# Block-sparse attention with a routed expert layer, one core: weights and next keys loaded at other steps, first loads reordered, the last pair staggered by three units, expert pieces moved

## The chip, the cores and the metric

The kernel runs on 1 core of one Trainium2 chip. The metric is the device time of one execution in microseconds (us). The engines are TensorE (PE; its weight loads are listed apart as PEld), VectorE (DVE), ScalarE (ACT), GpSimd (POOL) and SyncE (SP), and SP issues most transfers; its queue is listed as SPq.

## The reference

```
attention: B=4, H=8, S=768, D=64, blocks of 32 (24 blocks)
mask[i, j] = |i - j| <= 1 or i or j in {first, last block} or j in the 3 sampled blocks of i
x = softmax(scale * q k^T where mask) @ v          -> x[b] is 768 x 512 (all heads side by side)
routed expert layer, for each b, capacity 128:
  score = x[b] @ w_gate                            768 scores
  top   = the 128 rows with the largest score
  out[b]      = x[b]
  out[b, top] = x[b, top] + sigmoid(score[top]) * (relu(x[b, top] @ w1) @ w2)    w1 512x1024, w2 1024x512
```

## The kernel before

**Steps.** The batch elements are worked in two pairs (`n` = 0 and 1: b = 0, 1 and b = 2, 3). The list `steps` holds 56 steps, 28 for a pair. The first six of a pair are the "g" steps, three for each element: the first and the last block row, which see all keys (`s_g`, `pt_g`, `o_g`). Then come 11 units `u` (two block rows each), each unit once for either element: scores from the unit's own keys (`s<-k`), from gathered sampled keys (`s<-kr`), a maximum on DVE (`mx`), exponentials on ACT (`pr`), transposes on PE (`pt`, copied to `pc`), and the product with the values (`o<-vs`, `o<-vr`), normed on DVE (`x`) and written out. In step s the program issues: what `todo` holds for s (loads, gathers), due pieces "a", the norm of step s-1, exponentials of s+1, transposes of s, scores of s+2, the product `o` of s, due pieces "b", the maxima of s+2, then "c" and "d". Every engine runs its instructions in the order in which they are written.

**Transfers.** SP's queue carries queries (`load_q`), keys (`load_k`), values (`load_vs`, `load_vg`), outputs and the expert weights `w1_s`, `w2_s` (`w_load`, eight loads of 512 KB). POOL gathers the sampled value rows (`vr<-vt,vidx`, an indirect transfer) and copies sampled keys (`kr<-k`). `scale_q` multiplies a loaded query tile by 0.125 on ACT.

**Routing and experts.** For each element, `route(b)` lays down pieces at steps counted from `ready(t)`, the step after the one that ends score tile t (two units, 128 tokens): scores to a row (`row`, `row_out`, by way of DRAM and `spread`, or for the last tile on chip by a product with ones, `on_chip`), columns, six ranks `M` on DVE, `sums`, `select`, `chosen`, and `fetch`, which gathers the 128 chosen rows (`xe<-out,it` on POOL). The expert is `xt` (transposes), four plus four pieces `h_mm`, two `relu`, eight pieces `y_mm` and `put` (scatter to the output). `EXPERT[b]` says at which step `xt` stands. Steps above 55 hold no attention; there the pieces run one behind the other. In the last pair the final two units are staggered: both of b=2 first, then both of b=3.

```
    EXPERT = (38, 47, 2 * (NU - 1 + NG) + 33, 2 * (NU - 1 + NG) + 42)
    steps += [(B - 2 + i, u) for i in range(2) for u in (NU - 2, NU - 1)]
        early(9 + 2 * i, lambda i=i: w_load(i))
```

Of the kernel before, what the change touches and what calls it, by code (L numbers as in the profile page):

```python
# [7 lines left out]
F32 = mybir.dt.float32  # L8
# [22 lines left out]
NG = 3  # L31
# [14 lines left out]
def block_sparse_attention_moe(ctx, tc, qt, kt, vt, blocks, w_gate, w1, w2, outs):  # L46
# [61 lines left out]
    def load_vg(n, m):  # L108

        i, c = m // 3, m % 3  # L110
        if m % 2 == 0:
            vts[n, m // 2] = value_tile(f"vg{n}_{m}")
        vg = vts[n, m // 2][:, m % 2]
        cols = slice(i * VR, (i + 1) * VR)
        r = rows_of(n, 1 + 8 * c)
        if c < 2:
            sp.dma_start(vg, vt[r:r + 256, cols].rearrange("(m p) c -> p m c", p=P))
        else:
            sp.dma_start(vg[:, 0], vt[r:r + 128, cols])
            sp.dma_start(vg[0:64, 1], vt[r + 128:r + 192, cols])  # L120
            for k, j in enumerate((0, NB - 1)):
                r = rows_of(n, j)
                sp.dma_start(vg[64 + 32 * k:96 + 32 * k, 1], vt[r:r + BLK, cols])
# [23 lines left out]
                 blocks.bitcast(I32).rearrange("(o a) b -> o (a b)", o=1).broadcast_to([P, NB * 6]))  # L147
    load_k(0, 8, 16, 0, 1)
    load_k(0, 16, 24, 0, 1)
    load_vg(0, 0)  # L150
    load_q(0, 0, 1, 2)
    load_k(0, 0, 8, 1, 2)
    load_vg(0, 1)
    load_k(0, 8, 16, 1, 2)
    load_vg(0, 2)
    load_k(0, 16, 24, 1, 2)
    load_vg(0, 3)


# [273 lines left out]
    def small_t(shape, name):  # L433

        n = 1
        for c in shape[1:]:
            n *= c
        if spare["at"] + n > 512:
            spare["bank"], spare["at"] = ps_o.tile([P, 512], F32, tag="o", name=name), 0
        r = spare["bank"][:, spare["at"]:spare["at"] + n]  # L440
        spare["at"] += n + n % 2
        return r[0:shape[0]] if len(shape) == 2 else r.rearrange("p (a b) -> p a b", a=shape[1])[0:shape[0]]

    EXPERT = (38, 47, 2 * (NU - 1 + NG) + 33, 2 * (NU - 1 + NG) + 42)

    def route(b):
        R = {}
# [2 lines left out]
        def ready(t):  # L450
            return steps.index((b, 2 * t + 1)) + 1
# [22 lines left out]
        def on_chip():  # L474
            r = rout.tile([P, 2, 2 * BLK], F32, tag="r", name=f"r{b}")
            vec.tensor_tensor(r, sps[b][:, NU - 2:NU].unsqueeze(2).broadcast_to([P, 2, 2 * BLK]),
                              d64.unsqueeze(1).broadcast_to([P, 2, 2 * BLK]), ALU.mult)
            R["rp"] = small_t([P, P], f"rs{b}")
            pe.matmul(R["rp"], ones, r.rearrange("p u c -> p (u c)"), start=True, stop=True, skip_group_check=True)

        def on_chip_out():
            act.copy(R["sb"][:, S - P:S], R["rp"])

        def columns(t0, t1):
            R["scp", t0] = small_t([P, t1 - t0, BLK], f"scp{b}_{t0}")
            for t in range(t0, t1):
                pe.transpose(R["scp", t0][:, t - t0], R["sb"][0:BLK, t * P:(t + 1) * P], ident[0:BLK, 0:BLK])
# [55 lines left out]
            vec.reciprocal(ge, ge)  # L543

        def mid(name):
            return ps_m.tile([P, 512], F32, tag="m", name=f"{name}{b}").rearrange("p (t c) -> p t c", t=4)

        def xt():
            R["pm"] = mid("xt")
# [18 lines left out]

        def y_mm(f):
            if f == 0:  # L570
                R["y"] = ps_m.tile([P, 512], F32, tag="m", name=f"y{b}")
            pe.matmul(R["y"], R["h"][:, f], w2_s[:, f], start=f == 0, stop=f == 7)

        def put():
# [15 lines left out]
        c, r = ready(4) + 4, ready(5)  # L590
        last = b >= B - 2
        plan += [(c, "c", lambda: rank(3)), (c + 1 if last else c + 2, "c", lambda: rank(4))]
        plan += [(r, "b", on_chip), (r + 1, "a", on_chip_out), (r + 1, "b", lambda: columns(5, 6)),
                 (r + 2, "a", lambda: columns_out(5, 6)), (r + 2, "d", table)]
        c = r + 2 if last else r + 6
        plan += [(c, "c", lambda: rank(5)), (c + 1, "b", sums), (c + 1, "c", select), (c + 2, "b", chosen),
                 (c + 3, "a", fetch)]
        e = EXPERT[b]
        plan += [(e, "b", xt), (e + 1, "a", xt_out)]
        plan += [(e + 1 + c // 2, "b", lambda c=c: h_mm(c)) for c in range(4)]  # L600
        plan += [(e + 3, "a", lambda: relu(0))]
        plan += [(e + 3 + c // 2, "b", lambda c=c: h_mm(4 + c)) for c in range(4)]
        plan += [(e + 5, "a", lambda: relu(1))]
        plan += [(e + 5 + f // 2, "b", lambda f=f: y_mm(f)) for f in range(8)]
        plan += [(e + 9, "a", put)]
# [21 lines left out]
    def early(s, f):
        todo.setdefault(max(s, 0), []).append(f)
# [41 lines left out]
    for s in range(n + 1):  # L670
        for f in todo.pop(s, []):
            f()
        run(s, "a")
        done = None
        if s:
            t = steps[s - 1]
            if t[1] == "g":
                join(t[0], t[2])
            if t[1:] == ("g", NG - 1):
                done = (t[0], 0)  # L680
            elif t[1] != "g":
                done = t
        if done:
            norm(*done)
        if s < n:
            if s + 1 < n:
                exps(steps[s + 1], 0)
            turn(steps[s])
        if done:
            gate(*done)  # L690
        if s < n:
            if s + 1 < n:
                exps(steps[s + 1], 1)
            if s + 2 < n:
# [12 lines left out]
        run(s, "d")  # L707
# [43 lines left out]
```

## Time and profile before

| | |
|---|---|
| runs, us | 349.74 median of 3 (352.0, 349.74, 345.66) |
| profiled execution, us | 347.55, of which the span of instructions is 345.8 |
| busy, share of the span | PE 82%, PEld 62%, DVE 53%, ACT 47%, POOL 37% |
| transfers | 64.85 MB, 188 GB/s over the span |
| granted TensorE clock | 0.948 of full on average |

A step is seen on PE by its eight transposes `pt`: step 0's begin at 14.82 us, step 6's at 44.82, step 9's at 55.76, step 19's at 105.23, step 28's (the second pair) at 142.09, step 37's at 182.00, step 55's at 281.66. The last product `o` of step 55 ends at 284.62 us; what follows is the tail: the rest of routing for b = 2 and 3, and their two experts.

### The profile page before, as it was taken

To read this page: it belongs to the slowest core of one execution; us is meant where nothing else is said; L and a number is where in the kernel's file an instruction comes from. 1 tells how busy PE (TensorE), PEld (TensorE's weight loads), DVE (VectorE), ACT (ScalarE), POOL (GpSimd) and SP (SyncE) were. 2 spreads that over 40 slices of the span, in tenths; PEclk is the share of its full clock that TensorE was granted. 3 is DMA by queue.
4 is the path that set the end of the run, shared out by engine and by line. 5 is a ranking of instruction groups with operands and counts; after the bars stand their busy time and mean duration, and the time that the engine had idled before them with its cause. 6 is when DMAs were issued, how large, how long until landed. Compare 5 with 4: busy or idle time off the path is not lost.

```text
span 345.8 us, 13626 instructions
## 1 busy us (share of the span) xinstructions
PE 284.8 (82%) x5766; PEld 214.3 (62%) x5766; DVE 184.5 (53%) x536; ACT 161.2 (47%) x373; POOL 127.4 (37%) x271
## 2 busy tenths in 40 slices
PE   5597697799658889987879899998999983399791
PEld 4265576667546667766656788665788661384650
DVE  1756486466535777887876454544665627400000
ACT  2436676557446666595636554544464430100100
POOL 3129365565551400379637535523600004300101
PEclk9999699989989999999999999999999997579997
DMA  6999989988998984968947947645720211100000
GB/s 176 324 301 279 329 220 303 333 278 271 312 316 227 332 270 137 334 193 248 322 125 213 252 148 212 165 124 176 228 66 17 64 32 48 61 0 2 30 0 31
DMA packets 34541, 64.85 MB, mean 188 GB/s; under 512 B 4400, under 2 KB 18224, under 8 KB 34480
## 3 DMA queue, kind: packets, MB, share of 16 engines
q1 hardware_dynamic: 27504, 38.45, 38.5%
q0 software_dynamic: 6976, 25.53, 23.2%
q8 instruction: 45, 0.74, 0.9%
q14 instruction: 16, 0.13, 0.1%
HBM read 56.61 MB, written 7.35 MB: 185 GB/s over the span
## 4 chain that ended last, share of the span: by engine, by line
PE 44%; issue 25%; POOL 7%; DVE 7%; DMA 6%; SPq 5%; POOLq 3%; ACT 2%; DVEq 0%; ACTq 0%
PE o L69 14%; PE s L69 10%; PE pt L69 8%; POOL kr L69 5%; SPq L69 5%; PE h L69 5%; PE y L69 4%; DMA vg<-vt 3%; POOLq L263 2%; DMA q<-qt 2%; POOL vr L69 2%; DVE M L69 2%; PE o_g L69 1%; DMA xe<-out,it 1%; DVE gm L69 1%
## 5 line engine op out<-in xcount | busy, mean ns | idle before, releaser
L69 ACT ACTIVATE pr<-s,mx 128x256 f32<-128x256 f32 x176 | 74.7, 484 | 27.1 <-DVE mx L69 24.4
L69 DVE TENSOR_REDUCE mx<-s 128x2 f32<-128x512 f32 x88 | 56.8, 686 | 47.4 <-PE s L69 46.2
L69 POOL DMA_INDIRECT vr<-vt,vidx x44 | 43.0, 977 | 97.3 <-PE o L69 49.4
L69 POOL COPY kr<-k 128x256 f32 (+1 forms) x176 | 67.1, 423 | 16.1 <-DMA vg<-vt 9.0
L69 ACT COPY pc<-pt 128x512 f32<-128x512 f32 x78 | 42.5, 590 | 39.0 <-PE pt L69 38.7
L69 PE MATMUL pt<-ident,pr 128*128 128x128 f32 x352 | 47.6, 278 | 1.8 <-issue 1.8
L69 PE MATMUL s<-kr,q 64*32 64x128 f32 x1408 | 35.9, 284 | 9.5 <-issue 9.5
L69 PEld LDWEIGHTS pt<-ident,pr 128*128 128x128 f32 x352 | 38.4, 141 | 6.3 <-issue 3.8
L69 PE MATMUL o<-vr,pc 128*32 128x65 f32 x1408 | 32.2, 227 | 7.5 <-issue 7.5
L69 PE MATMUL h<-xT,w_s 128*128 128x128 f32 x256 | 34.1, 293 | 2.8 <-ACT h L69 1.4
L69 PE MATMUL o<-vs,pc 128*64 128x65 f32 x704 | 32.6, 232 | 3.5 <-ACT pc L69 1.4
L69 PEld LDWEIGHTS h<-xT,w_s 128*128 128x128 f32 x256 | 31.8, 204 | 5.2 <-ACT xT L69 2.0
L69 POOL DMA_INDIRECT out<-xe,it x4 | 4.0, 1006 | 83.1 <-DVE z L69 44.4
L69 PEld LDWEIGHTS o<-vs,pc 128*64 128x64 f32 x704 | 25.8, 141 | 13.8 <-ACT pc L69 4.5
L69 PEld LDWEIGHTS s<-kr,q 64*32 64x32 f32 x1408 | 20.5, 108 | 20.6 <-issue 20.5
L69 PE MATMUL y<-w_s,h 128*128 128x512 f32 x64 | 30.1, 609 | 1.4 <-ACT h L69 1.4
L69 PEld LDWEIGHTS o<-vr,pc 128*32 128x32 f32 x1408 | 23.7, 112 | 11.1 <-issue 7.9
L69 PE MATMUL s<-k,q 64*64 64x128 f32 x704 | 30.2, 288 | 0.2 <-issue 0.2
L69 DVE SCALAR_TENSOR_TENSOR xe<-y,ge,xe 128x512 f32<-128x512 f32 x4 | 3.0, 751 | 43.0 <-PE y L69 43.0
L69 PEld LDWEIGHTS s<-k,q 64*64 64x64 f32 x704 | 19.4, 135 | 7.7 <-issue 7.0
L69 DVE CUSTOM_DVE_ANT_0 j<-x,wg_i 128x256 f32<-128x256 f32 x48 | 22.5, 468 | 1.3
L69 PE MATMUL o_g<-vg,pc_g 128*64 128x65 f32 x384 | 15.1, 236 | 8.2 <-ACT pc_g L69 8.2
(115 smaller groups left out, 293.3 us busy)
## 6 DMA issues: line engine op xcount, KB each, us to landing
k<-kt SPq DMA_DIRECT2D x12, 512.0 KB
q<-qt SPq DMA_DIRECT2D x23, 256.0 KB
vs<-vt SPq DMA_DIRECT2D x22, 260.0 KB
out<-x SPq DMA_DIRECT2D x88, 64.0 KB
vg<-vt SPq DMA_DIRECT2D x8, 520.0 KB
w_s<-w SPq DMA_DIRECT2D x8, 512.0 KB
vs<-vt SPq DMA_DIRECT2D x12, 130.0 KB
vg<-vt SPq DMA_DIRECT2D x4, 260.0 KB
```

Of the source, the lines that this page charges most:

```text
L69: i = getattr(self.engine, name)(*args, **kw)
L263: _, offs[n, u] = nc.values_load_multi_w_load_instructions(koff[0:1, 2 * u - 1:2 * u + 1, :], engines=[POOL], min_val=0, max_val=(NB - 1) ...
```

## The change

Six things are done. (1) The eight weight loads go from steps 9, 11, ..., 23 to steps 29, 31, 33, 35, 36, 38, 40, 42. (2) The next pair's keys are loaded in eight pieces at steps 6, 8, ..., 20 in place of six at 8, 11, ..., 23. (3) In the first loads, the second query half goes ahead of the first values, the last keys and `load_q(0, 1)` ahead of the third values; `scale_q` goes from the head of a step, four steps ahead of its unit, to a place behind the exponentials, three ahead. (4) In the last pair three units are staggered (`AHEAD = 3`), and for b = 2 and 3 score tile 4 goes on chip like tile 5, tile 3 alone by DRAM; some ranks move. (5) Expert pieces of b = 0 and 1 stand at `xt` steps 35 and 48 (38 and 47 before), one `h_mm` a step in place of two. (6) The experts of b = 2 and 3 take their PSUM tiles from the four buffers of `ps_s` in place of the single one of `ps_m`.

```diff
+AHEAD = 3
     load_k(0, 16, 24, 0, 1)
+    load_q(0, 0, 1, 2)
     load_vg(0, 0)
-    load_q(0, 0, 1, 2)
     load_k(0, 0, 8, 1, 2)
     load_vg(0, 1)
     load_k(0, 8, 16, 1, 2)
+    load_k(0, 16, 24, 1, 2)
+    load_q(0, 1)
     load_vg(0, 2)
-    load_k(0, 16, 24, 1, 2)
     load_vg(0, 3)
...
-    EXPERT = (38, 47, 2 * (NU - 1 + NG) + 33, 2 * (NU - 1 + NG) + 42)
+    EXPERT = ((35, 1), (48, 1), (60, 2), (69, 2))
...
+            pool = (ps_s, "s") if b >= B - 2 else (ps_m, "m")
...
-        for t0, t1, lag in ((0, 3, 3), (3, 5, 2)):
+        for t0, t1, lag in ((0, 3, 3), (3, 4, 3)) if last else ((0, 3, 3), (3, 5, 2)):
...
+        for t in (4, 5) if last else (5,):
+            r = ready(t)
+            plan += [(r, "b", lambda t=t: on_chip(t)), (r + 1, "a", lambda t=t: on_chip_out(t)),
+                     (r + 1, "b", lambda t=t: columns(t, t + 1)), (r + 2, "a", lambda t=t: columns_out(t, t + 1))]
...
-        plan += [(e + 1 + c // 2, "b", lambda c=c: h_mm(c)) for c in range(4)]
+        plan += [(e + 1 + c // g, "b", lambda c=c: h_mm(c)) for c in range(4)]
...
-    steps += [(B - 2 + i, u) for i in range(2) for u in (NU - 2, NU - 1)]
+    steps += [(B - 2 + i, u) for i in range(2) for u in range(NU - AHEAD, NU)]
...
-            early(max(a - 4, k + 1), lambda n=n, u=u: scale_q(n, u))
+            scaled(max(a - 3, k + 1), lambda n=n, u=u: scale_q(n, u))
...
-            for c in range(6):
-                early(s0 - 20 + 3 * c, lambda n=n, c=c: load_k(n, 4 * c, 4 * c + 4))
+            for c in range(8):
+                early(s0 - 22 + 2 * c, lambda n=n, c=c: load_k(n, 3 * c, 3 * c + 3))
...
-        early(9 + 2 * i, lambda i=i: w_load(i))
+        early((29, 31, 33, 35, 36, 38, 40, 42)[i], lambda i=i: w_load(i))
```

**SP's queue.** This is SP in the first pair before, at steps 8 to 11 (`k1` is the next pair's keys, `q0_6` the query tile of unit 6 of pair 0, `x1_1` unit 1 of element 1, `w1_s` the weights).

```order
L69 DMA q0_6_914<-qt 128x512
L69 DMA k1_916<-kt 128x1024
L69 DMA out1<-x1_1_921 64x256 x2
L69 DMA w1_s_209<-w1 128x1024
L69 DMA out0<-x0_2_1025 64x256 x2
L69 DMA vs1_85<-vt 64x1040
L69 DMA q0_7_1112<-qt 128x512
L69 DMA out1<-x1_2_1117 64x256 x2
L69 DMA k1_916<-kt 128x1024
L69 DMA w1_s_209<-w1 128x1024
```

And this is SP of the changed kernel at the head of the second pair, steps 29 to 33.

```order
L70 DMA w1_s_211<-w1 128x1024
L70 DMA vs2_86<-vt 64x1040
L70 DMA vs2_86<-vt 32x1040 x2
L70 DMA q1_3_2992<-qt 128x512
L70 DMA w1_s_211<-w1 128x1024
L70 DMA out2<-x2_0_3083 32x256 x4
L70 DMA vs0_84<-vt 64x1040
L70 DMA vs0_84<-vt 32x1040 x2
L70 DMA q1_4_3159<-qt 128x512
L70 DMA w1_s_211<-w1 128x1024
```

The weights have left the first pair's stretch and stand between the second pair's values and queries.

**PE in the tail.** Before, behind the last product `o3_11_11` (b = 3, unit 11) stands one pair of `y1` (expert of b = 1), then routing only, up to `xt2`.

```order
L69 MATMUL o3_11_11_5559<-vr1_11_4889,pc3_11_11_1_5555 32x65 x16
L69 MATMUL y1_5375<-w2_s_210,h1_5098 128x512 x2
L69 MATMUL o3_11_11_5559<-ident_137,sb2_4441 128x32
L69 MATMUL o3_11_11_5559<-ident_137,sb3_4543 128x32 x2
L69 MATMUL rs3_5606<-r3_5604,ones_142 128x128
...
L69 MATMUL xt2_5721<-ident_137,xe2_5671 128x128 x4
```

In the changed kernel the same place holds two `h_mm` of b = 1 and all its eight `y` pieces, with the sums and choices of b = 2 and 3 between them (left out here).

```order
L70 MATMUL o3_11_11_5564<-vr1_11_4884,pc3_11_11_1_5560 32x65 x16
L70 MATMUL h4_1_5461<-xT1_4998,w1_s_211 128x128 x4
L70 MATMUL o3_11_11_5564<-ident_139,sb3_4542 128x32
L70 MATMUL h4_1_5461<-xT1_4998,w1_s_211 128x128 x4
...
L70 MATMUL cp2_5617<-r3_5_5639,ones_144 128x128
L70 MATMUL y1_5651<-w2_s_212,h1_5377 128x512 x2
...
L70 MATMUL y1_5651<-w2_s_212,h1_5377 128x512 x4
...
L70 MATMUL y1_5651<-w2_s_212,h1_5377 128x512 x2
L70 MATMUL xt2_5714<-ident_139,xe2_5665 128x128 x4
```

So three `y` pairs and two `h_mm` have moved from ahead of the last product to behind it, and the choice of b = 3 stands behind `xt2` where it stood ahead.

**ACT at the start.** Before, the scaling of the second query tile `q0_1` stands ahead of the exponentials of step 3 and the copies of step 2 (the rows `pr0_g`/`pr1_g` are exponentials, `pc0_g` copies).

```order
L69 ACTIVATE pr0_g_2_1_352<-s0_g_2_1_275,gm0_226 128x256 x2
L69 ACTIVATE q0_1_248<-q0_1_248 128x512
L69 ACTIVATE pr1_g_0_0_399<-s1_g_0_0_355,gm1_382 128x256 x2
L69 COPY pc0_g_2_0_407<-pt0_g_2_0_402 128x512
L69 COPY pc0_g_2_1_414<-pt0_g_2_1_409 128x512
```

In the changed kernel the same place reads:

```order
L70 ACTIVATE pr0_g_2_1_352<-s0_g_2_1_275,gm0_228 128x256 x2
L70 ACTIVATE pr1_g_0_0_398<-s1_g_0_0_355,gm1_382 128x256 x2
L70 COPY pc0_g_2_0_406<-pt0_g_2_0_401 128x512
L70 COPY pc0_g_2_1_413<-pt0_g_2_1_408 128x512
...
L70 ACTIVATE pr1_g_1_1_498<-s1_g_1_1_419,gm1_382 128x256 x2
L70 ACTIVATE q0_1_102<-q0_1_102 128x512
```

The scaling has moved from ahead of the copies `pc0_g_2` to behind the exponentials of two later steps.

More of the change, by code (lines that the diff above doesn't have):

```diff
@@ L472, in spread, with on_chip, on_chip_out @@
             sp.dma_start(R["sb"][:, t0 * P:t1 * P], R["row", t0].broadcast_to([P, (t1 - t0) * P]))
-        def on_chip():
-            r = rout.tile([P, 2, 2 * BLK], F32, tag="r", name=f"r{b}")
-            vec.tensor_tensor(r, sps[b][:, NU - 2:NU].unsqueeze(2).broadcast_to([P, 2, 2 * BLK]),
+        def on_chip(t):
+            r = rout.tile([P, 2, 2 * BLK], F32, tag="r", name=f"r{b}_{t}")
+            vec.tensor_tensor(r, sps[b][:, 2 * t:2 * t + 2].unsqueeze(2).broadcast_to([P, 2, 2 * BLK]),
                               d64.unsqueeze(1).broadcast_to([P, 2, 2 * BLK]), ALU.mult)
-            R["rp"] = small_t([P, P], f"rs{b}")
+            R["rp"] = small_t([P, P], f"rs{b}_{t}")
             pe.matmul(R["rp"], ones, r.rearrange("p u c -> p (u c)"), start=True, stop=True, skip_group_check=True)
-        def on_chip_out():
-            act.copy(R["sb"][:, S - P:S], R["rp"])
+        def on_chip_out(t):
+            act.copy(R["sb"][:, t * P:(t + 1) * P], R["rp"])
         def columns(t0, t1):
@@ L545, in mid @@
         def mid(name):
-            return ps_m.tile([P, 512], F32, tag="m", name=f"{name}{b}").rearrange("p (t c) -> p t c", t=4)
+            pool = (ps_s, "s") if b >= B - 2 else (ps_m, "m")
+            return pool[0].tile([P, 512], F32, tag=pool[1], name=f"{name}{b}").rearrange("p (t c) -> p t c", t=4)
         def xt():
@@ L570, in y_mm @@
             if f == 0:
-                R["y"] = ps_m.tile([P, 512], F32, tag="m", name=f"y{b}")
+                R["y"] = mid("y").rearrange("p t c -> p (t c)")
             pe.matmul(R["y"], R["h"][:, f], w2_s[:, f], start=f == 0, stop=f == 7)
@@ L578, in put @@
                 in_=R["xe"][:], in_offset=None)
+        last = b >= B - 2
         plan = [(ready(2), "b", begin)]
-        for t0, t1, lag in ((0, 3, 3), (3, 5, 2)):
+        for t0, t1, lag in ((0, 3, 3), (3, 4, 3)) if last else ((0, 3, 3), (3, 5, 2)):
             s_ = ready(t1 - 1)
@@ L589, in route @@
         plan += [(c, "c", lambda: rank(0)), (c + 1, "c", lambda: rank(1)), (c + 2, "c", lambda: rank(2))]
[L590 to L598, printed above, removed]
-        plan += [(e, "b", xt), (e + 1, "a", xt_out)]
-        plan += [(e + 1 + c // 2, "b", lambda c=c: h_mm(c)) for c in range(4)]
[L601 to L605, printed above, removed]
+        for t in (4, 5) if last else (5,):
+            r = ready(t)
+            plan += [(r, "b", lambda t=t: on_chip(t)), (r + 1, "a", lambda t=t: on_chip_out(t)),
+                     (r + 1, "b", lambda t=t: columns(t, t + 1)), (r + 2, "a", lambda t=t: columns_out(t, t + 1))]
+        c = r + 2 if last else r + 5
+        if last:
+            plan += [(ready(3) + 5, "c", lambda: rank(3)), (ready(4) + 2, "c", lambda: rank(4))]
+        else:
+            plan += [(r + 3, "c", lambda: rank(3)), (r + 4, "c", lambda: rank(4))]
+        plan += [(r + 2, "d", table), (c, "c", lambda: rank(5)), (c + 1, "b", sums), (c + 1, "c", select),
+                 (c + 2, "b", chosen), (c + 3, "a", fetch)]
+        e, g = EXPERT[b]
+        plan += [(e, "b", xt), (e + 1, "a", xt_out)]
+        plan += [(e + 1 + c // g, "b", lambda c=c: h_mm(c)) for c in range(4)]
+        e += 1 + 4 // g
+        plan += [(e, "a", lambda: relu(0))]
+        plan += [(e + c // g, "b", lambda c=c: h_mm(4 + c)) for c in range(4)]
+        e += 4 // g
+        plan += [(e, "a", lambda: relu(1))]
+        plan += [(e + f // 2, "b", lambda f=f: y_mm(f)) for f in range(8)]
+        plan += [(e + 4, "a", put)]
         for o, where, f in plan:
@@ L617, in block_sparse_attention_moe @@
             steps += [(2 * n + i, "g", c) for c in range(NG)]
-        for u in range(1, NU - 2 if n == NPAIR - 1 else NU):
+        for u in range(1, NU - AHEAD if n == NPAIR - 1 else NU):
             steps += [(2 * n + i, u) for i in range(2)]
-    steps += [(B - 2 + i, u) for i in range(2) for u in (NU - 2, NU - 1)]
+    steps += [(B - 2 + i, u) for i in range(2) for u in range(NU - AHEAD, NU)]
     n_, per = len(steps), 2 * (NU - 1 + NG)
@@ L623, in block_sparse_attention_moe, with scaled @@
         route(b)
-    todo = {}
+    todo, late = {}, {}
+    def scaled(s, f):
+        late.setdefault(max(s, 0), []).append(f)
     def early(s, f):
@@ L648, in block_sparse_attention_moe @@
             k = max(a - 8, free(n, u, 4, 2, 1))
-            early(k, lambda n=n, u=u: load_q(n, u))
-            early(max(a - 4, k + 1), lambda n=n, u=u: scale_q(n, u))
+            if n or u > 1:
+                early(k, lambda n=n, u=u: load_q(n, u))
+            scaled(max(a - 3, k + 1), lambda n=n, u=u: scale_q(n, u))
         if n:
             early(s0 - 8, lambda n=n: load_q(n, 0))
-            early(s0 - 4, lambda n=n: scale_q(n, 0))
-            for c in range(6):
-                early(s0 - 20 + 3 * c, lambda n=n, c=c: load_k(n, 4 * c, 4 * c + 4))
+            scaled(s0 - 4, lambda n=n: scale_q(n, 0))
+            for c in range(8):
+                early(s0 - 22 + 2 * c, lambda n=n, c=c: load_k(n, 3 * c, 3 * c + 3))
         for m in range(0 if n else 4, 6):
@@ L693, in block_sparse_attention_moe @@
                 exps(steps[s + 1], 1)
+            for f in late.pop(s, []):
+                f()
             if s + 2 < n:
```

## The prediction

> **What bounds the kernel now.** I read the page's shares first, then the table of stretches, then PE's waits in each stretch, then the timeline of the places that the change touches.
>
> ```profile
> PE 284.8 (82%) x5766; PEld 214.3 (62%) x5766; DVE 184.5 (53%) x536; ACT 161.2 (47%) x373; POOL 127.4 (37%) x271
> q8 instruction: 45, 0.74, 0.9%
> ```
>
> PE is the busiest engine, but 82% is a mean over stretches with different limits. The stretches are cut at step starts (columns: window, length, busy time of each engine, granted clock, transfer share, GB/s).
>
> ```profile
> 55.76:105.23 49.47, 38.95 (x1051) 30.20 (x1045) 26.36 (x74) 27.78 (x64) 26.34 (x55) 0.93 0.94 303
> 105.23:142.09 36.86, 33.16 (x893) 25.64 (x889) 27.22 (x84) 23.52 (x53) 5.23 (x11) 1.00 0.77 245
> 142.09:182.00 39.91, 33.77 (x772) 25.99 (x771) 32.39 (x89) 24.45 (x60) 26.63 (x56) 1.00 0.79 241
> 182.00:213.00 31.00, 28.69 (x682) 23.43 (x679) 16.07 (x50) 17.50 (x41) 17.85 (x37) 1.00 0.74 212
> 213.00:284.62 71.62, 69.09 (x1402) 50.64 (x1391) 36.67 (x114) 35.12 (x80) 15.65 (x32) 1.00 0.40 111
> 284.62:299.91 15.29, 5.11 (x64) 3.16 (x65) 10.49 (x36) 0.67 (x3) 7.04 (x13) 0.66 0.16 49
> 299.91:345.84 45.93, 33.70 (x168) 23.95 (x168) 1.50 (x2) 3.56 (x6) 2.04 (x3) 0.87 0.05 18
> ```
>
> Four regimes are seen. From 55.76 to 105.23 us the transfers are nearly full (share 0.94) and PE idles. From 142 to 213 nothing is full. From 213 to the last product PE is (69.1 of 71.6 us). From 284.62 PE waits for routing for 15.3 us, then does two experts in 45.9.
>
> What a step costs on PE without disturbance is the distance of two transposes without a wait between them:
>
> ```profile
> 131.23 1.09 PE L69 MATMUL pt<-ident,pr 128*128 128x128 f32 x8
> 134.67 1.09 PE L69 MATMUL pt<-ident,pr 128*128 128x128 f32 x8
> ```
>
> That is 3.44 us. From 55.76 to 105.23 there are ten steps, 4.95 each. What PE waits for from step 6 to 28 (44.82 to 142.09; total us, times, longest):
>
> ```profile
> PE s L69 <- issue: 7.2, 5, 3.6
> PE o L69 <- issue: 5.4, 4, 2.4
> PE pt L69 <- issue: 1.8, 1, 1.8
> ```
>
> One such wait in the timeline, and the queue of instructions in the transfers of 98.6 to 101.0 us:
>
> ```profile
> 98.14 0.42 PE L69 MATMUL s<-kr,q 64*32 64x128 f32 x8
> 102.13 1.08 PE L69 MATMUL s<-kr,q 64*32 64x128 f32 x24 [3.56 <-issue]
> ```
>
> ```profile
> q8 instruction: 1, 0.02, 2.5%
> ```
>
> 14.4 us go on waits that no engine explains, and they fall in the midst of 32 equal matmuls (8, a pause of 3.56 us, 24). 11,532 PE instructions by 45 packets of queue q8 make 256 a packet, and the last row has one such packet in that very pause. So I read these waits as PE without instructions, because their packet comes late when the queues are full. At 102.13 the products also run slower (24 take 1.08 us; 32 take 0.67 undisturbed), the clock of 0.93.
>
> **The Trainium skill on this.** Its page "Runtime: NRT & Kernel Launch", section "Instruction fetch mechanics", says blocks of 256 instructions are fetched ahead and the fetch is hidden because dispatch is slower than the refill. The 256 agree with the count above; "hidden" doesn't agree with the 3.56 us pause that holds a packet. By that page of the Trainium skill the pauses would have another cause, and to move the weights would free none of them: a rival below, with its time.
>
> **A, first loads (0 to 44.82).**
>
> ```profile
> 22.69 0.87 ACT L69 ACTIVATE pr_g<-s_g,gm 128x256 f32<-128x256 f32 x2
> 26.22 0.63 ACT L69 ACTIVATE q<-q 128x512 f32<-128x512 f32 x1 [2.66 <-DMA q<-qt]
> 28.10 1.17 PE L69 MATMUL o_g<-vg,pc_g 128*64 128x65 f32 x32 [2.40 <-ACT pc_g L69]
> 14.21 2.29 ACT L69 ACTIVATE pr_g<-s_g,gm 128x256 f32<-128x256 f32 x6 [1.02 <-DVE gm L69]
> ```
>
> ACT stands 2.66 us for a query tile that nobody needs yet, and PE then 2.40 us for ACT's copy. With the tile loaded earlier and scaled later that goes; next is the values' transfer, in a stretch whose queues are full, so I take -2 (from -4 to 0). The other reordered load gains nothing: the first exponentials wait for DVE, not for that query half. Elsewhere the later scaling still leaves a step ahead of the scores.
>
> **B, weights and keys out of the first pair (steps 6 to 28).**
>
> ```profile
> w_s<-w SPq DMA_DIRECT2D x8, 512.0 KB
> L69 SPq DMA_DIRECT2D w_s<-w x8: 435/585/1263, 55.0 to 123.1; - x8
> ```
>
> All eight loads, 4.2 MB, are issued between 55.0 and 123.1 us. At 303 GB/s they are 13.8 us of full queues. From 55.76 to 105.23 15.0 MB moved; without five loads, and with the keys' smaller pieces (next to no difference), 12.5 MB remain, 41.2 us at 303 GB/s against a floor of 34.4 us of PE: -8. The stretch to 142.09 loses three weight loads and one key piece, some 2.2 of 9.0 MB; its late packets (3.7 us of waits, quoted under C) mostly go: -4. Sum -12. Bounds: the whole loss against nothing but 3.44 a step is 97.3 - 22 x 3.44 = 21.6 us; I take -17 as the far end, -4 (a third) as the near one. SP gives up eight issues of 0.59 us each in this stretch and takes them up later; it isn't the bound in either.
>
> **C, the same loads in steps 29 to 42 (142 to 213).** 9.6 + 6.6 MB moved there in 70.9 us; with 4.2 more it is 20.4 MB, 288 GB/s: it fits, but nearly full. The price lies between nothing and 13.8 us. The nearest rows are PE's unexplained waits from 105.23 to 142.09 (first two), and those already here, from 142.09 to 213.00 (last two):
>
> ```profile
> PE s L69 <- issue: 2.5, 2, 1.3
> PE o L69 <- issue: 1.2, 1, 1.2
> ```
>
> ```profile
> PE s L69 <- issue: 1.9, 4, 1.0
> PE o L69 <- issue: 1.9, 3, 1.0
> ```
>
> 3.7 us in 36.9 would be 7.1 in 70.9, where 3.8 are now; I take +4. Two waits are new: `xt` of b=0 stands in the step of its fetch, two steps nearer than before. In the first row the gather starts 2.06 us after its step's transposes (176.33):
>
> ```profile
> 178.39 0.97 POOL L69 DMA_INDIRECT xe<-out,it  x1 [7.14 <-DVE ts L69]
> 296.51 1.01 POOL L69 DMA_INDIRECT xe<-out,it  x1 [0.88 <-DVE rs L69]
> 299.91 1.11 PE L69 MATMUL xt<-ident,xe 128*128 128x128 f32 x4 [2.03 <-DMA xe<-out,it]
> ```
>
> With idle queues it landed 3.4 us after its start; so 5.5 us into the step, more with full queues, against `xt`'s turn after 3.4 to 5.7. Behind `xt` on PE stands the next step's transposes, and all that follows. And the first `h` needs the weight block issued one step earlier. Together +2 (0 to +5). C is +6 (0 to +12).
>
> **D, expert pieces out of the loop.** From step 28 to the last product PE is full or nearly so, so a piece that leaves it shortens it.
>
> ```profile
> 213.12 2.05 PE L69 MATMUL h<-xT,w_s 128*128 128x128 f32 x16
> 230.22 1.98 PE L69 MATMUL y<-w_s,h 128*128 128x512 f32 x4
> 283.95 0.67 PE L69 MATMUL o<-vr,pc 128*32 128x65 f32 x32
> ```
>
> A row is two pieces. Before, one `y` pair stands behind the last product (ended 284.62); now two `h` pieces and four pairs do: 3 x 1.92 + 2.0 = 7.8 us leave. The two extra on-chip products cost 0.4. So -7.4 (-9 to -4: DVE's ranks of b=2 are now in these steps, but DVE is busy 36.7 of 71.6 us).
>
> **E, the tail.** Its parts before:
>
> ```profile
> 295.41 0.70 PE L69 MATMUL rs<-one_b,M 128*128 128x1 bf16 x21 [1.08 <-DVE ts L69]
> 301.70 6.15 PE L69 MATMUL h<-xT,w_s 128*128 128x128 f32 x32 [0.67 <-ACT xT L69]
> 308.53 3.84 PE L69 MATMUL h<-xT,w_s 128*128 128x128 f32 x32 [0.69 <-ACT h L69]
> 313.06 7.13 PE L69 MATMUL y<-w_s,h 128*128 128x512 f32 x16 [0.69 <-ACT h L69]
> 321.04 0.66 PE L69 MATMUL xt<-ident,xe 128*128 128x128 f32 x4 [0.84 <-DVE xe L69]
> 338.70 0.75 DVE L69 SCALAR_TENSOR_TENSOR xe<-y,ge,xe 128x512 f32<-128x512 f32 x1 [17.72 <-PE y L69]
> ```
>
> Now, from the last product: PE has 2.0 (`h`) + 7.7 (four pairs) + 2 x 0.7 (sums) + 0.8 (on-chip product, choice) = 11.9 us ahead of `xt` of b=2, and about 0.7 of waiting for the gate of the last unit: 12.6 in place of 15.3. The chosen rows of b=2 come earlier than that (fetch at 6.4, landed at 9.8), since its last unit is one step earlier, so PE doesn't wait for them, and the routing of b=3, once bare, lies under `y` and the first expert. Then each expert is 0.66 + 0.72 (copy) + 2 x 3.84 + 7.13 = 16.2: with four buffers the second `h` half follows the first without the 0.69 us pause, and `y` starts while the second half is still in ACT. The 6.15 falls to 3.84, since PE no longer idles just before it (clock 0.66 there now). From 338.70 to the end stay 7.2. Sum 12.6 + 32.4 + 7.2 = 52.2, against 61.2: -9 (-11 to -4; the near end keeps the half clock and 2 us of waiting).
>
> **Sum.** -2 - 12 + 6 - 7.4 - 9 = -24.4, from the profiled execution's 347.55: **323 us**. That execution lies 2.2 under the median; the runs before scatter by 6 us, so I add nothing. About 2% is what a measurement of this kernel can tell from no change.
>
> **Rivals.** *The weights only change place.* C is a stretch as full as the one they left, and the pauses follow them: B -7, C +13, so 335 (331 to 345). For it: 288 GB/s is close to 303. Against: before, 435 GB/s were asked for there at PE's pace (15.0 MB in 34.4 us); now about 290 in both places. *The pauses aren't caused by transfers:* B and C's +4 vanish, 331; the packet in the pause speaks against it. (The Trainium skill's rule above is of this kind.) *All pauses go:* B -17, C +2, E -11, 311. *Slower:* the clock. If packets come over 3 us late at each fetch in steps 28 to 43, PE's clock stays low; 62.5 us of PE work at 6.15 / 3.84 = 1.6 is +37, so 360. It decides only if a pause like that of 102.13 comes with every packet; at share 0.94 the mean clock was still 0.93.
>
> **How the numbers follow.** Forecast 0.62 (own range 313 to 331), weights only change place 0.23 (0.05 of it above 342.7, that is within 2% of 349.74), fetch not caused by transfers 0.05, all pauses go 0.07, slower 0.03. Faster by over 2% is 0.62 + 0.18 + 0.05 + 0.07 = 0.92, within 2% 0.05, slower 0.03. The range 311 to 336 leaves out the far part of the second case, some of the fourth and the last.
>
> **What would show it.** Step 28 begins near 128 us, not 142 (A, B), with PE's unexplained waits of the first pair near 4 us, not 14; steps 29 to 43 show more of them; the last product ends near 269 (284.62 - 14 + 6 - 7.4); from there to the end 52 us at full clock, without pauses between the halves of `h`. Wrong would be the forecast if step 28 still began after 138 (B), or if `xt` of b=0 or the first `h` held PE for over 5 us (C).

## The result, and the profile after

The changed kernel takes **326.85 us** (median of 4 runs, 325.54 to 330.55) beside 350.87 for the kernel before on the same chip: ratio 0.9388, 95% interval 0.9228 to 0.9547. The medians are 24.0 us apart, and the time is within the forecast (323, range 311 to 336). The ratio is that of the quicker runs alone (325.54, 325.73 and 327.97 beside 345.66 and 349.74, on average 21.3 us apart), since some runs of either kernel are over 1.5% longer than its quickest, among them the profiled one of the changed kernel (330.55 us, span 328.8) and that of the second profile of the kernel before (361.5 us). The stretches of the sum behave quite differently from the forecast, and most of what follows is about that. Two more profiles of the changed kernel, from the experiments, stand beside the first in the table below.

The page's shares after:

```profile
PE 277.7 (84%) x5770; PEld 211.1 (64%) x5770; DVE 184.5 (56%) x540; ACT 163.2 (50%) x375; POOL 125.0 (38%) x271
q8 instruction: 45, 0.74, 0.9%
```

PE does the same work in a shorter span. The table of stretches of the changed kernel, cut where step 6 begins, where step 28 begins, where step 43 begins, and where the last product `o` ends (columns: window, length, busy time of PE, PEld, DVE, ACT, POOL, granted clock, transfer share, GB/s):

```profile
38.76:140.50 101.74, 84.99 (x2249) 65.59 (x2245) 62.12 (x182) 61.17 (x137) 40.45 (x81) 0.95 0.79 236
140.50:217.12 76.62, 62.73 (x1457) 50.35 (x1456) 51.29 (x141) 42.78 (x102) 43.98 (x92) 0.96 0.90 267
217.12:279.31 62.19, 60.58 (x1359) 46.12 (x1357) 38.23 (x121) 34.74 (x80) 16.44 (x36) 1.00 0.46 125
279.31:328.80 49.49, 40.97 (x258) 28.11 (x258) 9.51 (x31) 4.83 (x10) 6.31 (x10) 0.97 0.10 32
```

The same cuts in a second profile of the kernel before, taken with the experiments:

```profile
41.67:155.43 113.76, 91.51 (x2248) 70.90 (x2245) 62.46 (x183) 60.30 (x136) 39.28 (x81) 0.89 0.81 249
155.43:230.12 74.69, 65.26 (x1465) 52.58 (x1464) 49.88 (x142) 41.93 (x101) 44.67 (x92) 0.98 0.73 214
230.12:299.43 69.31, 67.13 (x1373) 48.87 (x1371) 35.35 (x108) 35.11 (x80) 15.88 (x31) 1.00 0.40 109
299.43:359.80 60.37, 37.91 (x232) 26.20 (x232) 12.00 (x38) 4.23 (x9) 9.08 (x15) 0.86 0.08 26
```

All profiles of the two kernels side by side, in us:

| stretch | before, first profile | before, second | changed | changed, second | changed, third |
|---|---|---|---|---|---|
| start to step 6 | 44.8 | 41.7 | 38.8 | 38.4 | 38.4 |
| steps 6 to 28 | 97.3 | 113.8 | 101.7 | 101.4 | 103.6 |
| steps 28 to 43 | 72.9 | 74.7 | 76.6 | 80.3 | 77.5 |
| step 43 to the last `o` | 69.6 | 69.3 | 62.2 | 65.8 | 66.5 |
| tail | 61.2 | 60.4 | 49.5 | 49.6 | 49.6 |

Two things are to be seen. The tail and the stretch ahead of it gave most of the gain, in every profile (13.6 to 19.1 us). And the stretch of steps 6 to 28 differs by 16.5 us between two executions of *the same program before*; the first profile, on which the prediction was built, was a quick one there. 7.2 of these 16.5 us lie in steps 6 to 9, which took 10.9 us in the first profile of the kernel before, 18.2 in its second, and 17.3, 20.0 and 19.1 in the changed kernel. What PE waits for from step 6 to 28 in the changed kernel (total us, times, longest):

```profile
PE s L70 <- issue: 11.9, 6, 3.2
PE o L70 <- issue: 3.7, 3, 2.2
PE pt L70 <- issue: 1.1, 1, 1.1
```

That is 16.7 us of waits that no engine explains, where 4 were forecast and 14.4 stood before. From step 28 to 43 (the largest, and the new wait for the gathered rows):

```profile
PE o L70 <- issue: 6.2, 2, 4.1
PE o_g L70 <- issue: 3.3, 1, 3.3
PE s L70 <- issue: 2.3, 2, 1.5
...
PE xt L70 <- DMA xe<-out,it: 0.4, 1, 0.4
```

The tail of the changed kernel in the timeline (start, duration, instruction, idle time before and what ended it):

```profile
291.94 7.41 PE L70 MATMUL h<-xT,w_s 128*128 128x128 f32 x64 [0.54 <-ACT xT L70]
299.19 7.03 PE L70 MATMUL y<-w_s,h 128*128 128x512 f32 x16
306.05 0.60 PE L70 MATMUL xt<-ident,xe 128*128 128x128 f32 x4
307.38 7.41 PE L70 MATMUL h<-xT,w_s 128*128 128x128 f32 x64 [0.73 <-ACT xT L70]
314.63 7.03 PE L70 MATMUL y<-w_s,h 128*128 128x512 f32 x16
```

The 64 products `h` of an expert are one row now, without the pause between halves, and `y` follows without one.

### The profile page after: what moved, and what is told of

Read it like the earlier page. It is cut to its first block, busy times and chain, and to the rows that moved or that the text cites. A ratio compares the mean times of both kernels' runs of the same rounds, so it can differ in the third digit from the quotient of the medians.

```text
span 328.8 us, 13663 instructions
## 1 busy us (share of the span) xinstructions
PE 277.7 (84%) x5770; PEld 211.1 (64%) x5770; DVE 184.5 (56%) x540; ACT 163.2 (50%) x375; POOL 125.0 (38%) x271
## 3 DMA queue, kind: packets, MB, share of 16 engines
q0 software_dynamic: 6976, 25.53, 24.4%
## 5 line engine op out<-in xcount | busy, mean ns | idle before, releaser
L70 POOL COPY kr<-k 128x256 f32 (+1 forms) x176 | 66.1, 418 | 13.0 <-issue 7.1
L70 PE MATMUL pt<-ident,pr 128*128 128x128 f32 x352 | 49.7, 285 | 1.8 <-issue 1.8
L70 PE MATMUL s<-kr,q 64*32 64x128 f32 x1408 | 32.8, 281 | 13.3 <-issue 13.3
L70 PEld LDWEIGHTS pt<-ident,pr 128*128 128x128 f32 x352 | 40.3, 146 | 5.8 <-issue 2.6
L70 PE MATMUL o<-vs,pc 128*64 128x65 f32 x704 | 31.4, 232 | 1.8 <-ACT pc L70 0.7
L70 PEld LDWEIGHTS s<-kr,q 64*32 64x32 f32 x1408 | 18.7, 107 | 21.3 <-issue 20.8
L70 PEld LDWEIGHTS h<-xT,w_s 128*128 128x128 f32 x256 | 29.9, 191 | 3.1 <-ACT xT L70 1.6
L70 ACT ACTIVATE pr_g<-s_g,gm 128x256 f32<-128x256 f32 x48 | 20.0, 486 | 4.0 <-DVE gm L70 4.0
L70 ACT ACTIVATE q<-q 128x512 f32<-128x512 f32 (+1 forms) x25 | 15.6, 625 | 8.9 <-DMA q<-qt 8.9
L70 PEld LDWEIGHTS o_g<-vg,pc_g 128*64 128x64 f32 x384 | 13.1, 144 | 10.0 <-ACT pc_g L70 4.5
```

The lines of the kernel that those rows point to most:

```text
L70: i = getattr(self.engine, name)(*args, **kw)
```

## The experiments

Three groups of four kernels ran, each group on one chip. The kernel before measured 353.93, 352.39 and 353.71 us there (median of 7 runs each). Group 2 holds no run of the changed kernel; its kernels are compared with it by their ratios and, stretch by stretch, with its profiles of groups 1 and 3.

| | kernel | median us | ratio to before, 95% interval |
|---|---|---|---|
| 1 | the changed kernel | 334.66 | 0.9452 (0.9401 to 0.9502) |
| 1 | weights early | 333.38 | 0.9401 (0.9303 to 0.9499) |
| 1 | start as before | 332.90 | no interval |
| 1 | experts as before | 343.88 | no interval |
| 2 | fewer gathers | 318.28 | 0.9044 (0.8931 to 0.9158) |
| 2 | one PSUM tile | 340.32 | 0.9633 (0.9522 to 0.9744) |
| 2 | stagger two | 336.73 | 0.9524 (0.9407 to 0.9642) |
| 2 | later still | 330.94 | 0.9402 (0.9312 to 0.9493) |
| 3 | the kernel before | 358.15 | no interval |
| 3 | keys as before | 337.34 | 0.9480 (0.9364 to 0.9596) |
| 3 | keys later | 335.93 | 0.9493 (0.9393 to 0.9592) |
| 3 | the changed kernel | 335.55 | 0.9401 (0.9274 to 0.9529) |

**The changed kernel, again.** No edit.

> The changed kernel once more, as the base of the others. Theory (pauses of PE are late instruction packets, their number and length depends on what transfers run beside them): the head of step 28 comes between 132 and 141 us, with 8 to 16 us of unexplained PE waits from step 6 to 28; the stretch from the last product to the end is 49.5 us again, since no transfer disturbs it. Rival (the first profile is typical in every stretch): step 28 at 140.5 within 1 us, time 330.

334.66 us. Step 28 begins at 139.87 us with 15.9 us of unexplained waits ahead of it, at the far end of the theory's range and within the rival's as well. Its stretches (the column "changed, second" of the table above) are the base of this group.

**Weights early.** Only the weights go back to the first pair.

```diff
-        early((29, 31, 33, 35, 36, 38, 40, 42)[i], lambda i=i: w_load(i))
+        early(9 + 2 * i, lambda i=i: w_load(i))
```

> The changed kernel with the eight weight loads back at steps 9, 11, ..., 23. Theory: the loads cost where queues are full. Steps 6 to 28 get 4 to 12 us longer than in the changed kernel, steps 28 to 43 get 3 to 6 shorter, the time 1 to 6 us longer. Rival A (the place of the weights doesn't matter, pauses are not from transfers): both stretches unchanged within 2 us, time the same. Rival B (weights hurt the second pair more than they helped the first): time 2 to 5 us shorter than the changed kernel.

The changed kernel in the second profile, steps 6 to 28 and 28 to 43, and then the kernel with the weights early, the same:

```profile
38.43:139.87 101.44, 85.57 (x2248) 65.74 (x2244) 61.94 (x182) 60.71 (x137) 39.58 (x81) 0.95 0.83 238
139.87:220.21 80.34, 67.83 (x1457) 54.14 (x1456) 50.75 (x141) 42.87 (x102) 46.14 (x92) 0.92 0.87 259
```

```profile
38.10:147.16 109.06, 90.01 (x2248) 69.02 (x2245) 62.01 (x182) 60.93 (x137) 39.66 (x81) 0.92 0.87 265
147.16:219.28 72.12, 63.65 (x1457) 50.72 (x1455) 50.51 (x140) 42.90 (x102) 45.88 (x92) 0.98 0.77 216
```

In this pair of profiles the weights cost 7.6 us in the stretch where they stand early (109.06 against 101.44) and 8.2 where they stand late (80.34 against 72.12). Against all three profiles of the changed kernel it is 5.5 to 7.6 and 4.5 to 8.2 us, and the weights early have one profile only. Part of the price is waits (18.8 us unexplained against 15.9 in the first stretch, 4.2 against 9.4 in the second), part is the granted clock (0.92 against 0.95, and 0.98 against 0.92), at which the same products keep PE busy 4.4 us longer and 4.2 us shorter. The sums to step 43 are 219.28 and 220.21 us, and the time, which was to be 1 to 6 us longer, doesn't differ by more than the scatter. **To move the weights is worth nothing that these runs can tell**; they take their price along.

**Start as before.** The first loads in the old order, and every query tile loaded and scaled as before.

```diff
-    load_q(0, 0, 1, 2)
     load_vg(0, 0)
+    load_q(0, 0, 1, 2)
...
-    load_k(0, 16, 24, 1, 2)
-    load_q(0, 1)
     load_vg(0, 2)
+    load_k(0, 16, 24, 1, 2)
...
-            if n or u > 1:
-                early(k, lambda n=n, u=u: load_q(n, u))
+            early(k, lambda n=n, u=u: load_q(n, u))
-            scaled(max(a - 3, k + 1), lambda n=n, u=u: scale_q(n, u))
+            early(max(a - 4, k + 1), lambda n=n, u=u: scale_q(n, u))
```

> The changed kernel with the first loads in the order of before, and the query scaling back at the head of a step, four steps ahead. Theory: step 6 begins 4 to 6 us later (near 44 in place of 39), and of that 0 to 5 us reach the end, since the steps behind step 6 were slow in the changed kernel with full queues. Rival (the start only hands its gain to full queues): step 6 later by 5, step 12 and the end unchanged within 1 us.

The first two stretches of this kernel, and then those of the changed one (cut at steps 6 and 9):

```profile
0.00:40.49 40.49, 29.10 (x458) 20.76 (x458) 22.32 (x67) 19.84 (x48) 18.52 (x53) 1.00 0.98 278
40.49:60.47 19.98, 13.94 (x316) 10.55 (x312) 9.18 (x25) 8.57 (x20) 9.32 (x18) 0.83 0.90 252
```

```profile
0.00:38.43 38.43, 27.98 (x459) 20.64 (x459) 23.55 (x67) 19.46 (x47) 17.85 (x53) 0.82 0.97 276
38.43:58.45 20.02, 14.26 (x316) 10.80 (x312) 9.18 (x25) 8.34 (x20) 10.14 (x20) 0.83 1.00 242
```

Step 6 begins 2.06 us later with the old order, just the -2 of the prediction, and not the 4 to 6 us expected here; in the eleven profiles with the new order it begins at 37.7 to 38.8 us. But three steps then take 20 us either way, and at step 12 (70.92 with the old start; 72.48, 67.99 and 70.67 in the three profiles of the changed kernel) the 2 us are lost in the scatter. The time is 332.90 against 334.66. The 2 us are real at their place, and nothing shows that they reach the end.

**Experts as before.** The pieces of the experts of b = 0 and 1 at their old steps, two `h` pieces a step.

```diff
-    EXPERT = ((35, 1), (48, 1), (60, 2), (69, 2))
+    EXPERT = ((38, 2), (47, 2), (60, 2), (69, 2))
```

> The changed kernel with the expert pieces of b=0 and 1 where they were before (xt at 38 and 47, two h pieces a step). Theory: 7.8 us of PE work return ahead of the last product, which comes 7 to 8 us later (near 286 us), and the tail gets 0 to 3 us shorter, since its routing chain is bare again: the time is 5 to 8 us longer. Rival (PE isn't the bound in the loop): the last product moves by under 3 us and the time by under 2.

Slower: by 9.2 us in the medians (343.88 against 334.66), whose runs scatter by as much (339.27 to 348.37), and by 5.8 us between the two profiled executions (343.03 against 337.26). The last stretch ahead of the tail and the tail, and the tail's first expert:

```profile
218.50:288.92 70.42, 68.43 (x1379) 49.91 (x1377) 38.11 (x119) 36.02 (x83) 16.26 (x36) 1.00 0.39 108
288.92:341.30 52.38, 37.53 (x230) 27.17 (x230) 9.51 (x31) 4.23 (x9) 6.35 (x10) 0.84 0.09 30
```

```profile
300.11 1.12 PE L70 MATMUL xt<-ident,xe 128*128 128x128 f32 x4 [1.32 <-DMA xe<-out,it]
301.90 9.92 PE L70 MATMUL h<-xT,w_s 128*128 128x128 f32 x64 [0.53 <-ACT xT L70]
```

The loop is 4.6 us longer (70.42 against 65.81), the tail 2.8 (52.38 against 49.58), where 7 to 8 us and a shorter tail were expected. With only one pair of `y` left behind the last product, PE waits for routing there, and comes to the first `h` at a lower clock (0.50 from 295.0 to 301.9 us): 9.92 us for what takes 7.41. So the pieces moved behind the loop do two things: they leave a stretch where PE is full, and they keep PE at work where it waited.

**Fewer gathers.** Are the unexplained waits caused by transfers at all? Here the largest of them are left out: the value rows of units 5 to 11 of the first pair.

```diff
-            vrs[n, u] = value_tile(f"vr{n}_{u}")
+            vrs[n, u] = value_tile(f"vr{n}_{u}") if n or u <= 4 else vrs[0, 4]
...
-        pool.indirect_dma_start(
+        if n or u <= 4:
+            pool.indirect_dma_start(
```

> The changed kernel without the value rows that POOL gathers for units 5 to 11 of the first pair (unit 4's rows are used in their place, 14 gathers of 0.53 MB left out). Theory (PE's unexplained waits are instruction packets that come late behind transfers): these waits fall from 16 us to under 6 between steps 6 and 28, that stretch from 102 to 80-88 us, and the time by 12 to 20 us. Rival (the waits have another cause, as the skill's page on instruction fetch would have it): at least 12 us of them stay and the stretch stays over 96 us.

From step 12 to 28 in this kernel, the stretch and then PE's waits in it; then the changed kernel, the same:

```profile
67.40:126.70 59.30, 58.03 (x1626) 45.06 (x1621) 44.82 (x137) 44.04 (x99) 13.80 (x39) 1.00 0.61 172
```

```profile
PE s L70 <- issue: 1.0, 1, 1.0
PE o L70 <- issue: 0.2, 1, 0.2
```

```profile
72.48:139.87 67.39, 59.27 (x1626) 45.56 (x1620) 45.59 (x137) 43.76 (x99) 24.68 (x51) 1.00 0.76 228
```

```profile
PE s L70 <- issue: 5.2, 4, 2.5
PE o L70 <- issue: 2.7, 3, 1.1
PE pt L70 <- issue: 0.3, 1, 0.3
```

1.2 us of unexplained waits in place of 8.2, and 59.30 us in place of 67.39. Steps 6 to 28 took 88.9 us with 8.5 of waits, just above what was expected (80 to 88, under 6): the gathers of units 1 to 4 are still there up to step 12, and so are the waits. PE issues the same instructions in both, so the waits come with the gathers. What this run alone doesn't tell is whether it is their bytes, their many packets or POOL's work of issuing them (24.68 us of POOL against 13.80). Steps 28 to 43 say more: POOL's work is the same there with and without the weights (46.14 and 45.88 us), and the unexplained waits are 3.8, 4.2 and 4.5 us in the three profiles without the weight loads in that stretch, 5.8 to 12.5 us in the eleven with them. So plain loads cause such waits too. By the ratio the time fell by some 13 to 14 us, where 12 to 20 were expected.

**One PSUM tile.** The last two experts get the single buffer back.

```diff
-            pool = (ps_s, "s") if b >= B - 2 else (ps_m, "m")
+            pool = (ps_m, "m")
```

> The changed kernel with the experts of b=2 and 3 back on the single PSUM tile. Theory: the four pauses of 0.69 us between the halves and ahead of y come back, and the 0.75 us of put ahead of the second expert with its wait, so the stretch from the last product to the end is 3.5 to 5 us longer than 49.5. Rival (PE was held elsewhere): under 1.5 us longer.

Its tail's second expert, in the timeline (the last row is its successor):

```profile
306.37 3.84 PE L70 MATMUL h<-xT,w_s 128*128 128x128 f32 x32 [0.75 <-ACT h L70]
310.90 7.13 PE L70 MATMUL y<-w_s,h 128*128 128x512 f32 x16 [0.69 <-ACT h L70]
318.88 0.66 PE L70 MATMUL xt<-ident,xe 128*128 128x128 f32 x4 [0.85 <-DVE xe L70]
```

The rows are the second half of `h` of b = 2, its `y`, and `xt` of b = 3. The pauses of 0.75, 0.69 and 0.85 us return and the tail is 55.6 us, 6.1 more (3.5 to 5 were expected). From one `xt` to the next it is 18.4 us (300.46 to 318.88) where the changed kernel takes 15.4 (290.66 to 306.05): the three pauses are 2.3 of it, and the rest is in somewhat longer rows. The four buffers are worth about 6 us: wherever the tail was left alone it took 49.5 to 49.6 us, in seven profiles (48.5 in *fewer gathers*).

**Stagger two.** Two units staggered, as before.

```diff
-AHEAD = 3
+AHEAD = 2
```

> The changed kernel with two staggered units in place of three (the on-chip ranks and the expert places stay). Theory: the chosen rows of b=2 come one step later, so behind the 11.9 us of PE work that now hide them only in part: the stretch behind the last product is 0 to 3 us longer, the loop the same. Rival (the stagger is what made the tail shorter): 5 us or more longer.

In its tail, whose last product ends at 282.21, POOL's gather of b = 2 and PE's first expert:

```profile
292.30 1.02 POOL L70 DMA_INDIRECT xe<-out,it  x1 [0.88 <-DVE ge L70]
...
295.71 0.65 PE L70 MATMUL xt<-ident,xe 128*128 128x128 f32 x4 [1.30 <-DMA xe<-out,it]
```

The gather begins 10.1 us into the tail (6.3 in the changed kernel), `xt` waits 1.30 us for it, and the first `h` then takes 9.04 us in place of 7.41. The tail is 53.4 us, 3.8 more. The expectation had the wait, not the lower clock behind it (0.83 from 295.7 to 306.0 us). The ratio alone (0.9524, interval 0.9407 to 0.9642) does not tell this kernel from the changed one; the tail does.

**Later still.** Weights, keys and the first experts each some steps later.

```diff
-        early((29, 31, 33, 35, 36, 38, 40, 42)[i], lambda i=i: w_load(i))
+        early((34, 36, 37, 38, 40, 42, 44, 46)[i], lambda i=i: w_load(i))
...
-    EXPERT = ((35, 1), (48, 1), (60, 2), (69, 2))
+    EXPERT = ((39, 1), (52, 2), (60, 2), (69, 2))
...
-                early(s0 - 22 + 2 * c, lambda n=n, c=c: load_k(n, 3 * c, 3 * c + 3))
+                early((12, 14, 16, 18, 20, 22, 23, 24)[c], lambda n=n, c=c: load_k(n, 3 * c, 3 * c + 3))
```

> The changed kernel with weights at steps 34 to 46, xt of b=0 and 1 at 39 and 52 (two h pieces a step for b=1), and the next keys at steps 12 to 24. Theory (PE waits follow the transfers): steps 6 to 19 get 3 to 8 us shorter, steps 28 to 43 lose 3 to 6 us of unexplained waits, the tail grows by the 2 us of PE work moved into it, and the time falls by 2 to 8 us. Rival (transfers only change place again): the waits turn up at steps 19 to 28 and 34 to 46 and the time is the same within 2 us.

330.94 us, ratio 0.9402: no difference from the changed kernel that these runs can tell (0.9388 to 0.9452 in its three measurements). Steps 6 to 28 take 98.4 us and 28 to 43 73.6, together the least of all profiles of kernels with the change that leave nothing out; but what moved from there stands in the next two stretches, 67.9 and 51.1. The work changed place, and the 2 to 8 us that were expected did not come.

**The kernel before, again.** No edit.

> The kernel before once more, for the spread of its stretches. Theory (the first profile of before had a quick first pair; weights there cost 7 us): steps 6 to 28 take over 100 us here, step 6 comes at 40 to 45, steps 28 to 43 take 71 to 74, the tail 59 to 62. Rival (the first profile is typical): steps 6 to 28 take 97 us within 1.5.

Its profiled execution took 361.5 us; its rows stand in the first section. Its unexplained waits in steps 6 to 28 are 18.3 us (14.4 in the first profile), and PE is busy for 91.5 us there (82.8) at a clock of 0.89 (0.96).

**Keys as before, and keys later.** Only the pieces of the next pair's keys.

```diff
-            for c in range(8):
-                early(s0 - 22 + 2 * c, lambda n=n, c=c: load_k(n, 3 * c, 3 * c + 3))
+            for c in range(6):
+                early(s0 - 20 + 3 * c, lambda n=n, c=c: load_k(n, 4 * c, 4 * c + 4))
```

> The changed kernel with the next keys in six pieces at steps 8 to 23. Theory (only how much is asked for while queues are full matters): steps 6 to 9 get 0 to 2 us shorter, steps 19 to 28 0 to 2 longer, the time the same within 3 us. Rival (the keys' early pieces are what gives the weights' gain back): steps 6 to 28 shorter by 5 us or more.

```diff
-                early(s0 - 22 + 2 * c, lambda n=n, c=c: load_k(n, 3 * c, 3 * c + 3))
+                early((12, 14, 16, 18, 20, 22, 23, 24)[c], lambda n=n, c=c: load_k(n, 3 * c, 3 * c + 3))
```

> The changed kernel with the next keys in its eight pieces at steps 12 to 24. Theory: steps 6 to 12, full of transfers, get 1 to 3 us shorter, and steps 12 to 28 stay, so the time falls by 0 to 4 us. Rival (nothing is won, the transfers only change place): the same within 1 us, steps 19 to 28 longer by what steps 6 to 19 gain.

Steps 6 to 28 take 105.5 us with the old pieces and 103.0 with the later ones, against 103.6 in the changed kernel of the same group; 337.34, 335.93 and 335.55 us in all. The keys' places decide nothing that can be measured.

**The changed kernel, a third time.** No edit.

> The changed kernel, as the base of the two others on the same chip. Theory: its ratio to the kernel before is 0.935 to 0.95, steps 6 to 28 take 99 to 103 us, the stretch from the last product to the end 49.5 us. Rival (its ratio depends on the chip): outside 0.93 to 0.955.

335.55 us; its profile is the last column of the table.

## Why the prediction was right, and where it wasn't

The time came out within the range although B failed, A was lost within six steps and D was mostly smaller than forecast. A, B and C together were forecast at -8 us, and undoing them one by one shows about nothing. D and E together were forecast at -16.4, and the two last stretches gained 13.6 to 19.1. So the larger half of the sum held, and the shortfall of the other half fell inside the range: that 326.85 lies so near to 323 is in part luck. By the three ratios the gain is 19 to 21 us, not 24.4.

| term | forecast | measured | by |
|---|---|---|---|
| A, first loads | -2 | -2.1 at step 6, not to be told by step 12 | start as before |
| B, weights and keys out of steps 6 to 28 | -12 | weights -5.5 to -7.6, keys nothing sure | weights early, keys as before |
| C, into steps 28 to 43, two new waits | +6 | weights +4.5 to +8.2 | weights early |
| D, expert pieces out of the loop | -7.4 | -3.0, -3.6 and -7.3 | three profiles against 69.45, the mean of two |
| E, tail | -9 | -10.8 to -11.7 | 60.4 and 61.2 against 49.5 |

**B is the step that failed.** It took steps 9 to 19 as bounded by bytes: 12.5 MB left, 41.2 us at 303 GB/s. The bytes did go as reckoned: 11.88 MB moved in that stretch of the changed kernel, at a share of 0.85. But it took 46.0 us, and PE's unexplained waits in it were 9.2 us, against 10.5 before. Steps 19 to 28 took 38.4 us, where 36.9 stood and 32.9 were forecast. The row of steps 9 to 19:

```profile
56.05:102.09 46.04, 36.68 (x1052) 28.17 (x1045) 26.51 (x74) 27.68 (x62) 25.98 (x54) 1.00 0.85 258
```

A share under one did not free PE. Where these waits fall is seen when the second profile of the changed kernel is cut at the ends of successive pauses:

```profile
63.63:79.51 15.88, 14.56 (x380) 11.36 (x380) 9.36 (x27) 10.10 (x23) 9.72 (x20) 0.89 0.86 258
79.51:84.66 5.15, 4.37 (x128) 3.34 (x128) 3.51 (x9) 3.23 (x8) 2.64 (x6) 1.00 0.83 228
84.66:89.67 5.01, 4.24 (x127) 3.30 (x127) 2.66 (x8) 3.69 (x9) 2.12 (x5) 1.00 0.91 328
89.67:94.62 4.95, 4.66 (x127) 3.60 (x127) 3.35 (x9) 2.17 (x5) 3.69 (x7) 1.00 0.91 275
94.62:100.65 6.03, 4.92 (x127) 3.62 (x128) 3.71 (x13) 4.98 (x11) 3.63 (x9) 1.00 0.79 236
100.65:107.45 6.80, 4.33 (x127) 3.26 (x128) 2.39 (x7) 3.06 (x7) 2.41 (x6) 1.00 0.93 261
107.45:117.54 10.09, 8.96 (x254) 7.05 (x255) 8.25 (x25) 6.07 (x14) 4.96 (x10) 1.00 0.81 263
117.54:130.90 13.36, 13.12 (x382) 10.27 (x382) 10.51 (x35) 10.34 (x23) 0.00 (x0) 1.00 0.51 145
```

The first two counts in brackets are PE's and PEld's instructions: 254 to 256 together in five rows, and two or three times as many in the others (509, 760, 764). So the pauses stand at the ends of blocks of 256 instructions, as the prediction read them, but they come at shares from 0.79 up, not only when the transfers are full; and at 0.81 and 0.86 some blocks end without one. In the last row, at a share of 0.51, three blocks go by before the next wait, and that is one of 0.24 us. I read from it that less transfer makes these waits rarer, but that the mean share of a stretch alone doesn't set them; the weights' 4.2 MB were too little for B, the 14 gathers of 0.53 MB in *fewer gathers* (share 0.61) were not. (The Trainium skill, page "Runtime: NRT & Kernel Launch", section "Instruction fetch mechanics", calls the crossing of such a block mostly hidden; the rows of several blocks agree in part, the five of one block don't, and here the measurement decides.)

**The rivals.** *The weights only change place* was right in its mechanism and in B (-7 forecast, -5.5 to -7.6 measured). Its C of +13 was too large (+8.2 at most), and its 335 us had D and E as in the forecast, so the 19 to 21 us by the ratios lie between its -12.4 and the forecast's -24.4. The prediction's argument against it does not hold: it set 435 GB/s asked for before against about 290 after, but 290 is a mean over steps 9 to 28. In steps 9 to 19, for which the 435 stand, the 12.5 MB left in 34.4 us are 363 GB/s, still above the 303 that flowed there. *The pauses aren't caused by transfers* is refuted by fewer gathers. *All pauses go* is refuted by the 16.7 us that stayed (its terms add up to 312 us, not 311). *Slower by the clock* did not come as a whole, but the clock of steps 28 to 43 fell from 1.00 and 0.98 to 0.92 to 0.96, and that is a part of C's price.

**C.** The two new waits were taken at 2 us. The gathered rows hold `xt` of b = 0 for 0.4 us, and no wait of the first `h` is seen. The rest is the weights' own price, in waits and in the clock.

**D and E are one exchange.** The profile of experts as before puts 4.6 us of the places' worth in the loop and 2.8 in the tail. The prediction had reckoned D at 7.4 and booked the covered routing to E. D came short because the work that left did not all become time: in the loop PE is busy for 68.4 of 70.4 us with the old places and for 62.2 of 65.8 with the new ones, so it stands idle for 1.6 us more. In eight other profiles of kernels with the new places the loop took 65.9 to 66.9 us; the 62.2 of the first profile is the exception. E itself went as worked out: `xt` of b = 2 begins 11.35 us into the tail (12.6 forecast), an expert takes 15.4 (16.2), the end 7.1 (7.2), at a clock of 0.97 (0.66 and 0.87 before). The experiments split the whole: about 7 us for the experts' places, 6 for the PSUM tiles, 4 for the stagger. That is 17 together, beside the 13.6 to 19.1 that the two last stretches gained and the 19 to 21 of the ratios; each was undone alone, by one profile each, so the sum is an estimate. Weights, keys and first loads add nothing that was measured. The on-chip scores of tile 4 were not undone.

**What would have shown it wrong.** Step 28 begins at 140.50 (139.87, 142.03), after the 138 that the prediction named as the mark against B. The last product ends at 279.31, not 269, and the tail takes 49.5, not 52.2.

## What to carry to other kernels

A load that is moved out of a crowded stretch into another one takes its price along; price it in both, and ask whether the second is any emptier in the way that counts. Work of PE that is ready and not urgent is best kept for the places where PE would wait: here it cost nothing there, and the clock stayed up for what followed. Before a term is built on one profile, compare a second one of the same program: here a single stretch differed by more than any term of the sum. And where a stretch is bounded by waits, price them as waits: fewer bytes did not shorten it in proportion.

## What the hardware showed that was not expected

The pauses of PE stand 254 to 256 of its instructions apart, or two or three times that, and last from 0.2 to over 4 us in stretches whose mean transfer share is 0.76 or more. The longest of the changed kernel's first profile fell in the midst of a row of 21 equal small sums (at 174.48 us):

```profile
169.72 0.61 PE L70 MATMUL o<-one_b,M 128*128 128x1 bf16 x19
174.48 0.19 PE L70 MATMUL o<-one_b,M 128*128 128x1 bf16 x2 [4.14 <-issue]
174.53 1.95 PE L70 MATMUL pt<-ident,pr 128*128 128x128 f32 x8
```

The eight transposes behind it took 1.95 us, 1.09 when undisturbed, and the granted clock from 174.5 to 176.5 us was 0.50: this pause was paid for again in the clock behind it.

A lower clock was seen behind shorter waits as well. In experts as before none of PE's waits between the last product and the first `h` was over 1.5 us, and the `h` took 9.92 us in place of 7.41; in stagger two the longest was 1.30, and it took 9.04. (The Trainium skill, page "TensorE: Matmul & The Clock Gate", section "HAM oscillation — how this bites in real kernels", warns of idle gaps over some 3.4 us; here shorter ones came ahead of a lower clock, 0.50 and 0.83.)
